# Seven ff tiles in the first pass instead of six, and a margin in the plan ahead of TensorE, in a fused attention and feed-forward kernel

## The chip, the core and the metric

The kernel runs on one NeuronCore of a Trainium2 chip. The metric is the device time of one execution in microseconds. The kernel before takes 1096.32 us, the median of three runs (1095.8 to 1097.32).

## What is computed

Eight batches of eight heads, 576 positions, head dimension 64: banded causal attention (a window of 128 keys) with a linear position bias, then a feed-forward layer over the 4608 tokens with 512 model columns and 2048 ff columns. All in float32.

```python
scores = scale * np.matmul(q, k.transpose(0, 1, 3, 2))
mask = (rel >= 0) & (rel < window)
scores = np.where(mask, scores + bias[None], -1000000000.0)
attn = np.exp(scores - max) / sum
x = (attn @ v).transpose(0, 2, 1, 3).reshape(B * S, H * D)
h = x @ w_in
sp = np.maximum(h, 0.0) + np.log1p(np.exp(-np.abs(h)))
out = (h * erf(sp)) @ w_out
```

## The kernel before

**Attention.** The 64 heads are 32 pairs, counted from 0 (`pair = 4 * batch + g`). A pair has five score groups (`QTILES`), three in its first span and two in its second; the first eight pairs do all first spans before the second ones. For each group TensorE makes the scores `s` (L520, plain fp32, in the early spans; L531, split operands, later), VectorE adds the bias and finds the row's extreme (`p<-s`, L542), ScalarE exponentiates (L552), VectorE inverts the sums (`st`, L570), GpSimd scales `p` (L577), TensorE transposes it (`t`, L595), VectorE or ScalarE copies it out of PSUM, TensorE multiplies it by the values (`px`, L613), and the result `xs` is stored to `xd` in DRAM, and for the first two chunks also kept on chip. Apart from the early first spans, which borrow two more, `s` has a single PSUM buffer: a score group can start only when VectorE has read the one before. The operands of a late pair are split into two parts first (`kh`, `kl`, `a`: L472 to L489) on VectorE, ScalarE and GpSimd.

**Feed-forward.** The tokens are 12 chunks of 384 columns, the 2048 ff columns 16 tiles of 128. One unit is one tile for one chunk: 12 products into `h` (L795), a copy to `hs`, the activation in rounds of four units on ScalarE (L826), the products and the split on VectorE (L836, L840), and 9 products into `o` (L855). There are 192 units. The output accumulates over the ff tiles, and not all weights fit on chip while attention runs, so there are two passes: the first takes the first `NF1` ff tiles for all chunks and stores its sums to DRAM; the second takes the rest, reads these sums back and adds them. The first pass is the filler between attention's instructions; its chunk can begin once attention has finished the batches that the chunk holds (chunk 9 needs batch 6; chunks 10 and 11 need batch 7). `xr` is the chunk loaded back, `xh` and `xl` its two parts (L777 to L781, L770).

**Weights.** Each ff tile of `w_in` and `w_out` arrives as 64-bit words (`wri`, `wro`) and is turned into two float32 parts (`whi`, `wli`, `who`, `wlo`) by a chain on ScalarE and VectorE (L684 to L704). Here "a weight tile" is one ff tile of one of the two. Those of the first pass are prepared while attention runs; those of the second live, all but two tiles of each, in the memory that attention gives back.

**The order.** Nothing is scheduled by the compiler. `Plan` lists every operation with its cost on the engines that could take it, an urgency `at` and its dependencies, walks through time, and hands each engine that is free the most urgent operation that is ready; that gives each engine its fixed order, which the chip then follows with semaphores. `hop` is the time that the planner lets pass between the end of an operation and the start of one that depends on it. `at` of a unit of the first pass grows by `TM` per unit, and `TM` is made from `NF1` such that the pass keeps its length: 4.80 us a unit with six tiles, 4.11 with seven. At the start, 40 small products on a zero tile (`warm`, L399) have the least urgency and fill TensorE's gaps.

Of the kernel before, what the change touches and what calls it, by code (L numbers as in the profile page):

```python
# [26 lines left out]
NTT = CH // P  # L27
LOG_EXP_SET = "natural_log_exp_and_others"

NF1 = 6  # L30
FIT = 8
UPR = (4, 4)
TAIL = (2, 2)
EARLY = 16
# [10 lines left out]
LL, LP, LT = 15, 6, 0  # L45
TM = 1.2 * TA * 20 / (1.5 * NF1)
LEAD = 70
# [84 lines left out]
class Plan:  # L132
# [7 lines left out]
    def hop(self, src, dst):  # L140
        if src == "PE":
            return 0.0 if "PE" in dst else 0.2
        return 0.2 if "Pool" in dst else 0.14

    def __init__(self):
        self.ops = []
# [562 lines left out]
class Moe:  # L709
# [4 lines left out]
    def __init__(self, tc, plan, ctx, x_dram, part_dram, out):  # L714
# [11 lines left out]
        self.rounds = []  # L726
        for n, size, tail in zip((NF1, NF - NF1), UPR, ((), TAIL)):
            n = n * nch - sum(tail)
# [157 lines left out]
def tile_kernel(ctx, tc, qT, kT, vb, w_in, w_out, bias, out, nb=B):  # L886
# [24 lines left out]

    n1 = nch * NF1
    t0 = LEAD
    t1 = t0 + n1 * TM
    w1 = Weights(nc, plan, lambda k, f: (w1p, f"{k}_{f}"), stage, w_in, w_out, range(NF1))
    for k in range(2):
        for f in range(NF1):
            w1.prepare(k, f, t0 - W1A + (f * W1C + W1B * k) * TM)
# [11 lines left out]
    for o in ops:  # L930
        o.outs.append(last)
    pool2 = lambda: w2p[0]
    place = lambda k, f: (
        (pool2, f"{k}_{f}") if f < NF1 + FIT else (w1p, f"{k}_{f - NF1 - FIT}")
    )
# [43 lines left out]
```

## Time and profile before

| | before |
|---|---|
| median of three runs | 1096.32 us |
| profiled execution | 1095.57 us |
| its span, first to last instruction | 1093.8 us |
| mean granted TensorE clock | 0.994 |
| DMA | 109.51 MB, 100 GB/s over the span |

A row of the table of stages reads: stretch in us, its length, then for TensorE (PE), its weight loads (PEld), VectorE (DVE), ScalarE (ACT) and GpSimd (POOL) the busy time and the count of instructions, then the granted TensorE clock, the share of the DMA engines and GB/s. A row of waits reads: engine, what waited and its line, what it waited for, total us, times, the longest. A row of the timeline reads: start, length, engine, line, operation, result and operands; in brackets the idle time ahead of it and what ended it. A busy TensorE is not one at its peak, since its products overlap in the record.

### The profile page before, as it was taken

The page shows a single profiled execution, that of the slowest core. Times are in us where ns is not written, and L with a number is a line of the kernel's source. Part 1 is how long each engine was busy: PE and PEld are TensorE (multiplying, and loading weights), DVE is VectorE, ACT ScalarE, POOL GpSimd, SP SyncE. Part 2 cuts the span into 40 slices and gives each one's busy share as a digit, 9 for nine tenths or more (in the row PEclk, how much of TensorE's full clock was granted, in tenths as well). Part 3 has the DMA queues.
Part 4 walks back from the last instruction along what each step waited for, and adds up shares of the span by engine and source line. Part 5 has one row for each costly group of instructions (what it writes and reads, how often), then busy time and mean ns, then how long its engine had stood idle before and what let it go on. Part 6 is the DMA issues. An engine that isn't in the chain of part 4 may idle for free.

```text
span 1093.8 us, 16894 instructions
## 1 busy us (share of the span) xinstructions
PE 1065.1 (97%) x6000; PEld 975.3 (89%) x6000; DVE 677.9 (62%) x1531; ACT 676.2 (62%) x1393; POOL 289.6 (26%) x438
## 2 busy tenths in 40 slices
PE   7998999999999989999999999999999999999998
PEld 7987889988999989899999998999999999999996
DVE  2789999878887787764888873433333334343342
ACT  4766887776777677765766663645535545445461
POOL 5645657565545555441100000000000000000000
PEclk9998999999999999999999999999999999999999
DMA  6553644646453453412434411220210210202102
GB/s 177 148 157 111 179 132 122 197 110 173 132 138 106 130 157 98 134 34 88 135 117 131 149 61 46 87 63 24 87 58 29 87 54 34 87 19 68 58 17 71
DMA packets 88260, 109.51 MB, mean 100 GB/s; under 512 B 45808, under 2 KB 58224, under 8 KB 88176
## 3 DMA queue, kind: packets, MB, share of 16 engines
q1 hardware_dynamic: 88176, 108.42, 33.6%
q8 instruction: 48, 0.79, 0.3%
q14 instruction: 36, 0.29, 0.1%
HBM read 80.08 MB, written 28.31 MB: 99 GB/s over the span
## 4 chain that ended last, share of the span: by engine, by line
PE 86%; DVE 5%; DMA 3%; POOL 3%; issue 1%; SPq 0%; ACT 0%; POOLq 0%; DVEq 0%
PE o L855 34%; PE h L795 34%; PE px L613 7%; PE t L595 5%; PE s L531 4%; POOL p L577 3%; PE s L520 2%; DMA xr<-xd 1%; DVE p L542 1%; DVE a_None L489 1%; DMA a<-q_t 1%; DMA kz<-k_t 1%; DMA wri<-w_in 1%; DVE hs L836 1%; DVE kl_None L486 0%
## 5 line engine op out<-in xcount | busy, mean ns | idle before, releaser
L795 PE MATMUL h<-xh,whi 128*128 128x384 f32 x768 | 263.9, 344 | 0.7 <-DVE xh L781 0.5
L795 PE MATMUL h<-xh,wli 128*128 128x384 f32 x768 | 260.0, 339 | 0.5 <-DVE wli L704 0.5
L795 PE MATMUL h<-xl,whi 128*128 128x384 f32 x768 | 259.1, 337 | 0.9 <-DVE xl L770 0.9
L855 PE MATMUL o<-who,gh 128*128 128x512 f32 x576 | 228.1, 396 | 0.0
L855 PE MATMUL o<-who,gl 128*128 128x512 f32 x576 | 227.5, 395 | 0.0
L855 PE MATMUL o<-wlo,gh 128*128 128x512 f32 x576 | 227.1, 394 | 0.0
L577 POOL TENSOR_SCALAR p<-p,st 128x256 f32<-128x256 f32 (+2 forms) x320 | 197.3, 635 | 95.2 <-DVE st L570 94.2
L777 ACT COPY hs<-h 128x384 f32<-128x384 f32 x113 | 53.8, 477 | 233.7 <-PE h L795 233.2
L552 ACT ACTIVATE p<-p,st 128x256 f32<-128x256 f32 (+2 forms) x320 | 149.0, 468 | 33.4 <-DVE st L542 32.9
L781 DVE COPY hs<-h 128x384 f32<-128x384 f32 x79 | 43.8, 555 | 192.6 <-PE h L795 192.4
L795 PEld LDWEIGHTS h<-xh,whi 128*128 128x128 f32 x768 | 145.4, 189 | 8.6 <-DVE xh L781 0.9
L795 PEld LDWEIGHTS h<-xl,whi 128*128 128x128 f32 x768 | 145.3, 189 | 7.5 <-DVE xl L770 1.1
L795 PEld LDWEIGHTS h<-xh,wli 128*128 128x128 f32 x768 | 144.8, 189 | 1.0 <-DVE wli L704 1.0
L542 DVE CUSTOM_DVE_ANT_0 p<-s,bias_sb 128x256 f32<-128x256 f32 (+2 forms) x320 | 108.8, 378 | 40.4 <-PE s L531 16.1
L855 PEld LDWEIGHTS o<-who,gl 128*128 128x128 f32 x576 | 108.0, 188 | 23.3
L855 PEld LDWEIGHTS o<-wlo,gh 128*128 128x128 f32 x576 | 108.3, 188 | 16.1
L855 PEld LDWEIGHTS o<-who,gh 128*128 128x128 f32 x576 | 108.4, 188 | 15.4
L836 DVE TENSOR_TENSOR hs<-s,hs 128x768 f32<-128x768 f32 x96 | 90.9, 970 | 23.6 <-ACT s L826 23.5
L840 DVE TENSOR_TENSOR gl<-hs,gh 128x768 fp32r<-128x768 f32 x96 | 90.8, 963 | 0.7 <-ACT gh L777 0.6
L595 PE MATMUL t<-ident,p 128*128 128x128 f32 x544 | 82.1, 276 | 6.6 <-POOL p L577 6.2
L595 PEld LDWEIGHTS t<-ident,p 128*128 128x128 f32 x544 | 64.6, 143 | 17.1 <-POOL p L577 9.8
L826 ACT ACTIVATE s<-s 128x768 f32<-128x768 f32 x96 | 76.0, 839 | 0.6
(78 smaller groups left out, 1486.3 us busy)
## 6 DMA issues: line engine op xcount, KB each, us to landing
xr<-xd SPq DMA_DIRECT2D x22, 768.0 KB, 4.3
kr_None<-k_t SPq DMA_DIRECT2D x48, 288.0 KB, 4.3
pd<-ot SPq DMA_DIRECT2D x36, 256.0 KB, 3.6
ot<-pd SPq DMA_DIRECT2D x36, 256.0 KB, 3.0
wri<-w_in SPq DMA_DIRECT2D x16, 512.0 KB, 4.3
wro<-w_out SPq DMA_DIRECT2D x16, 512.0 KB, 3.7
out_dram<-ot SPq DMA_DIRECT2D x32, 256.0 KB, 2.1
qr_None<-q_t SPq DMA_DIRECT2D x24, 288.0 KB, 4.3
```

Source lines behind the costliest of these rows:

```text
L542: nc.vector.tensor_tensor_reduce(out=pt[:m, c0:c1, j, :], in0=blocks(ps[:m, j, :n]), in1=blocks(self.bias[:m, c0 * 64 : c1 * 64]), scale=- ...
L552: nc.scalar.activation(dst, dst, AF.Exp, bias=low[:m, j : j + 1], scale=-1.0, accum_out=total[:m, j : j + 1],)
L577: nc.gpsimd.tensor_scalar(dst, dst, totals[t][:m, j : j + 1], 1.0, op0=ALU.mult, op1=ALU.mult)
L595: nc.tensor.matmul(ps[:, col : col + P], lhsT=p[t][:, kb].rearrange("p j d -> p (j d)"), rhs=self.ident[:, :], is_transpose=True, start=no ...
L613: self.nc.tensor.matmul(dst[:, q0 - base : q1 - base], lhsT=v[:, blk], rhs=sb[sbi][:, off : off + q1 - q0], start=(blk == order[0][0]), st ...
L777: self.nc.scalar.copy(out, src)
L781: self.nc.vector.tensor_copy(out, src)
L795: nc.tensor.matmul(ps[:, :CH], lhsT=ww[:, cs], rhs=xx[:, k], start=(k2 + k + n == 0), stop=(k2 + k + n == 4),)
L826: A.activation(s[:, :n], s[:, :n], AF.Erf)
L836: op({"DVE": dve(n2)}, lambda e, s=s, hs=hs, n=n: V.tensor_tensor(hs[:, :n], s[:, :n], hs[:, :n], ALU.mult), r=[s, hs], w=[hs], at=at)
L840: op({"DVE": dve(n2)}, lambda e, gh=gh, gl=gl, hs=hs, n=n: V.tensor_tensor(gl[:, :n], hs[:, :n], gh[:, :n], SUB), r=[hs, gh], w=[gl], at=at)
L855: nc.tensor.matmul(po.all, lhsT=g[:, j, cs], rhs=w.all, start=(u["start"] and n == 0), stop=(u["end"] and n == 2),)
```

## The change

`NF1` goes from 6 to 7, so the first pass has 84 units and the second 108 (72 and 120 before); 14 weight tiles are prepared under attention and 18 for the second pass (12 and 20). `FIT` goes from 8 to 7: seven ff tiles of the second pass lie in the memory that attention gives back, and two in the places of the first pass's tiles 0 and 1, as before. And the planner lets 0.6 us more pass between an operation of any other engine or a DMA and a TensorE operation that depends on it. The margin is in the plan alone; no instruction waits for it.

```diff
-NF1 = 6
-FIT = 8
+NF1 = 7
+FIT = 7
...
     def hop(self, src, dst):
         if src == "PE":
             return 0.0 if "PE" in dst else 0.2
-        return 0.2 if "Pool" in dst else 0.14
+        return 0.2 if "Pool" in dst else 0.14 + 0.6 * ("PE" in dst)
```

Every engine's order is new from its first rows on. Three places matter below. First TensorE, at the first two score groups of pair 26 (`s26_0`, `s26_1`, `s26_2` are its groups, `px24_1` a product of pair 24). Before, the third group comes directly behind the second:

```order
L613 MATMUL px24_1_4971<-pb24_4953,vbd0_160 128x64
L531 MATMUL s26_1_4983<-kh26_None_0_4759,a26_None_0_4783 128x256
L531 MATMUL s26_1_4983<-kl26_None_0_4836,a26_None_0_4783 128x256
L531 MATMUL s26_1_4983<-kh26_None_1_4785,a26_None_1_4806 128x256
L531 MATMUL s26_1_4983<-kl26_None_1_4852,a26_None_1_4806 128x256
L531 MATMUL s26_2_5010<-kh26_None_0_4759,a26_None_0_4783 128x256
```

and now transposes of pair 25 and products `o` follow the second group, and the third comes only behind a whole unit's `h`:

```order
L531 MATMUL s26_1_5206<-kl26_None_1_5007,a26_None_1_4956 128x256
L595 MATMUL t25_1_0_5213<-ident_62,p25_4_5111 128x128
L595 MATMUL t25_1_0_5213<-ident_62,p25_3_5081 128x128 x2
L595 MATMUL t25_1_0_5213<-ident_62,p25_4_5111 128x128
L595 MATMUL t25_1_0_5213<-ident_62,p25_3_5081 128x128
L855 MATMUL o1_35_4640<-who5_1794,gh40_4906 128x512
L855 MATMUL o1_35_4640<-wlo5_1807,gh40_4906 128x512
L855 MATMUL o1_35_4640<-who5_1794,gl40_4921 128x512
L855 MATMUL o2_35_4667<-who5_1794,gh40_4906 128x512
```

Second GpSimd, at the cast of chunk 9 (`xh9`), before:

```order
L577 TENSOR_SCALAR p28_4_5509<-p28_4_5509,st28_1_5474 128x3x64 x2
L779 TENSOR_SCALAR xh9_0_5693<-xr9_1_5635 128x768
L476 TENSOR_SCALAR a31_None_0_5712<-qr31_None_5601 64x576
L476 TENSOR_SCALAR kh31_None_1_5720<-kr31_None_5580 128x576
L476 TENSOR_SCALAR a31_None_1_5728<-qr31_None_5601 64x576
L779 TENSOR_SCALAR gh44_5762<-hs44_5427 128x768
```

and now:

```order
L476 TENSOR_SCALAR kh31_None_1_5964<-kr31_None_5788 128x576
L476 TENSOR_SCALAR a31_None_1_5976<-qr31_None_5810 64x576
L779 TENSOR_SCALAR xh9_0_5990<-xr9_1_5895 128x768
L577 TENSOR_SCALAR p29_3_5918<-p29_3_5918,st29_1_5919 128x4x64 x2
L577 TENSOR_SCALAR p29_4_5947<-p29_4_5947,st29_1_5919 128x3x64 x2
L779 TENSOR_SCALAR gh54_6091<-hs54_5812 128x768
```

The operands of pair 31 stood behind the cast and now stand ahead of it. Third VectorE near the start, behind the sixth score group (`p1_2`), before:

```order
L542 ISA p1_2_281,st1_0_260<-s1_2_263,bias_sb_63 128x4x64
L542 ISA st1_0_260 128x1
L570 RECIPROCAL st0_0_227<-st0_0_227 128x6
L542 ISA p2_0_308,st2_0_309<-s2_0_300,bias_sb_63 128x2x64
L542 ISA st2_0_309 128x1
```

and now, with the steps of the first weight tile (`wti0`, `wqi0`) between the two score groups:

```order
L542 ISA p1_2_280,st1_0_259<-s1_2_262,bias_sb_63 128x4x64
L542 ISA st1_0_259 128x1
L687 TENSOR_SCALAR wti0_290<-wqi0_232 128x512
L689 SCALAR_TENSOR_TENSOR wti0_290<-wqi0_232,wti0_290 128x512
L570 RECIPROCAL st0_0_226<-st0_0_226 128x6
L691 TENSOR_SCALAR wqi0_232<-wti0_290 128x512
L542 ISA p2_0_311,st2_0_312<-s2_0_300,bias_sb_63 128x2x64
```

## The prediction

> **What bounds the kernel now.** I read the page's totals first, then a table of stages, then the waits of TensorE, and last the chain of waits and the timeline at single stops.
>
> ```profile
> span 1093.8 us, 16894 instructions
> PE 1065.1 (97%) x6000; PEld 975.3 (89%) x6000; DVE 677.9 (62%) x1531; ACT 676.2 (62%) x1393; POOL 289.6 (26%) x438
> ```
>
> TensorE (PE) is busy for 97% of the span; what it waits for is at most 28.7 us. The stages come from the last attention product on TensorE and from a table with PE, weight loads, VectorE, ScalarE and GpSimd, then the granted clock:
>
> ```profile
> L613 PE MATMUL px<-pb,vbd x320: 218/275/377, 68.2 to 502.7; 128*128 128x64 f32 x64, 128*128 128x128 f32 x64, 128*128 128x192 f32 x32
> ...
> 0.00:60.00 60.00, 54.28 (x354) 51.69 (x354) 32.00 (x140) 35.62 (x133) 34.44 (x79) 0.97 0.57 155
> 60.00:100.00 40.00, 32.85 (x191) 28.98 (x190) 34.15 (x95) 27.04 (x71) 20.47 (x31) 0.92 0.56 152
> 100.00:150.00 50.00, 48.70 (x304) 45.20 (x303) 47.96 (x112) 38.78 (x93) 29.81 (x35) 1.00 0.52 148
> 150.00:503.00 353.00, 343.15 (x2225) 319.45 (x2224) 275.34 (x775) 255.94 (x706) 192.86 (x283) 1.00 0.46 127
> 503.00:1071.00 568.00, 568.00 (x2855) 515.35 (x2855) 283.96 (x406) 314.36 (x388) 11.97 (x12) 1.00 0.22 72
> ```
>
> Attention ends at 503 us. Behind it TensorE is busy for 568.00 of 568 us: nothing can be won there except by less work. Ahead of it PE sits idle 5.72, 7.15, 1.30 and 9.85 us, 24.0 in all, and the half clock costs a further 0.03 x 60 + 0.08 x 40 = 5.0 us there. The rest of the 28.7 is the tail, which ends in the same order as before. So a change of order can win at most some 29 us, all in the first 503.
>
> [...]
>
> **The part that is moved.** One unit is one ff tile of one chunk: 12 products h and 9 products o. In the chain of waits a unit looks like this (start, length, line, count):
>
> ```profile
> 700.21 2.10 PE h L795 x12
> 702.31 2.08 PE o L855 x9
> ```
>
> That is 2.10 + 2.08 = 4.18 us a unit, for 192 units before and after. How many lie inside attention now:
>
> ```profile
> 0.00:503.00 503.00, 136.35 (x660) 114.97 (x660) 0.99 0.48 134
> ...
> 0.00:503.00 503.00, 120.03 (x439) 76.33 (x440) 0.99 0.48 134
> ```
>
> The first row is L795, the second L855: 660 / 12 = 55 units of h and 439 / 9 = 48.8 of o. In the new order 756 and 504 products stand ahead of the last attention product, so 63 and 56 units. Inside attention that adds 8 x 2.10 + 7.2 x 2.08 = 31.8 us, and the same 31.8 us leave the stage behind it, which is full either way. **Term 1: 0 us.** Attention would end near 535 us. What could change is only how often TensorE stops on the way there, because the same attention work is now spread over 32 us more of filler.
>
> The changeover costs nothing either: 21 units (84 - 63) of the first pass remain behind attention, 17 before, so 87.8 us of cover instead of 71.1, and 18 weight tiles must be prepared under it instead of 20. If that cover failed, one late tile would hold a unit, 3.6 us of VectorE's time each, as worked out below.
>
> **The stops.** TensorE's waits from 100 to 503 us, and below the dots from 0 to 100 (total, times, longest):
>
> ```profile
> PE s L531 <- DVE st L542: 4.8, 2, 2.8
> PE t L595 <- POOL p L577: 4.5, 7, 1.3
> ...
> PE s L520 <- DMA kz<-k_t: 4.7, 1, 4.7
> PE s L520 <- DVE st L542: 3.4, 3, 1.8
> PE t L595 <- POOL p L577: 1.8, 3, 1.0
> PE s L520 <- issue: 1.4, 1, 1.4
> ```
>
> *Transposes waiting for GpSimd* (L595): 6.3 us in ten waits, 0.63 us each. The new margin lets a product be placed 0.6 us later behind its producer, so by size it could remove nearly all of them. I check that in the order: priced at the cadence of the rows (h 0.175 us a product, o 0.231, and likewise the rest), less than 8 us of TensorE work lies between a bank's last score and its transposes at 12 of 108 places of the old order behind the first 60 us, and at 8 of 111 of the new. A third fewer would be -2.1 us, all of them -6.3; were the delays of GpSimd larger than the margin, nothing or +1.5 (two more). **Term 2: -3 us**, nearer to the count, since the margin moves the plan and not the engines.
>
> *Score groups that follow one another on the one PSUM buffer* (L531, L520): the second must wait until VectorE has read the first. These stops in the timeline, with what ended them:
>
> ```profile
> 395.73 0.28 PE L531 MATMUL s<-kl_None,a_None 128*128 128x256 f32 x1
> 398.77 0.35 PE L531 MATMUL s<-kh_None,a_None 128*128 128x256 f32 x1 [2.76 <-DVE st L542]
> ...
> 92.04 0.89 PE L520 MATMUL s<-kz,a 128*128 128x192 f32 x4 [1.83 <-DVE st L542]
> 94.35 2.04 PE L520 MATMUL s<-kz,a 128*128 128x256 f32 x4 [1.43 <-issue]
> ...
> 76.94 0.89 PE L520 MATMUL s<-kz,a 128*128 128x192 f32 x4 [1.07 <-DVE st L542]
> ```
>
> Behind the first 60 us of that work the old order has three places where a group directly follows another on that buffer: the stops of 2.76, 1.43 and 1.07 us, 5.3 us in all, 1.75 each. At the place of 2.76 (pair 26) the new order has six products o and twelve h in between, 3.5 us, and transposes. But it has two such places of its own (pair 8 to 9, and pair 13). Two at 1.75 are 3.5; bounds 2 x 1.07 and 2 x 2.76. **Term 3: -1.8 us**, from -3.2 to +0.2.
>
> *A queue held up by a load.* The other stop of 150 to 503 us, with GpSimd's row, the load in the chain of waits, VectorE's row, and two windows with their clock:
>
> ```profile
> 447.11 7.62 DMA xr<-xd
> ...
> 454.88 0.83 POOL L779 TENSOR_SCALAR xh<-xr 128x768 fp32r<-128x768 f32 x1 [11.17 <-PE s L531]
> ...
> 456.38 1.21 DVE L489 TENSOR_TENSOR a_None<-qr_None,a_None 64x576 fp32r<-64x576 f32 x1 [2.37 <-POOL a_None L476]
> ...
> 458.27 0.36 PE L531 MATMUL s<-kh_None,a_None 128*128 128x256 f32 x1 [2.05 <-DVE st L542]
> ...
> 350.00:400.00 50.00, 47.06 (x309) 43.99 (x308) 40.74 (x119) 36.56 (x111) 29.82 (x47) 1.00 0.47 134
> 450.00:500.00 50.00, 47.95 (x295) 44.91 (x294) 28.82 (x83) 33.50 (x86) 23.98 (x37) 0.97 0.20 65
> ```
>
> GpSimd's cast of chunk 9 waits for a load of 7.62 us; behind it in its queue stands pair 31's query, for which VectorE waits with the bias of pair 30 behind it, and TensorE needs that buffer. It costs 2.05 us and 0.03 x 50 = 1.5 us of half clock. In the new order pair 31's operands stand ahead of the cast, and behind it the scaling of pair 29, which feeds transposes later on. All gone would be -3.5; the same wait elsewhere, 0. **Term 4: -2.5 us.** [...]
>
> **What is added.** First, two weight tiles more to prepare while attention runs, 14 instead of 12, on VectorE (min, median and longest in ns):
>
> ```profile
> L687 DVE TENSOR_SCALAR wti<-wqi x16: 386/418/843, 27.3 to 565.4; 128x512 int32<-128x512 int32 x16
> L689 DVE SCALAR_TENSOR_TENSOR wti<-wqi,wti x16: 677/684/741, 27.8 to 566.2; 128x512 int32<-128x512 int32 x16
> L691 DVE TENSOR_SCALAR wqi<-wti x16: 415/420/545, 33.3 to 567.7; 128x512 int32<-128x512 int32 x16
> L692 DVE SCALAR_TENSOR_TENSOR wqi<-wri,wqi x16: 650/684/714, 34.1 to 568.9; 128x512 f32<-128x512 uint32 x16
> L700 DVE TENSOR_TENSOR wti<-wti,wqi x16: 679/692/798, 37.7 to 569.6; 128x512 f32<-128x512 f32 x16
> L704 DVE TENSOR_TENSOR wli<-wti,whi x16: 672/684/860, 44.2 to 571.8; 128x512 fp32r<-128x512 f32 x16
> ...
> 19.81 0.29 DVE L542 CUSTOM_DVE_ANT_0 p<-s,bias_sb 128x128 f32<-128x128 f32 x1 [7.66 <-PE s L520]
> ```
>
> The six add up to 3.58 us a tile, 7.2 for two. VectorE is free for 5.9 us of 60 to 100 and for only 2.0 us of 100 to 150, so this is where it would hurt. Against that, the new order begins the first tile right behind the sixth score group, in the 7.66 us in which VectorE now waits for the seventh, and has all 14 done by the 47th score group, where the old one has 12 done by the 50th. One tile in the idle stretch leaves 3.6 us for the crowded part, against 7.9 us of room there. From -1 to +7.2; **term 5: +1 us**. The early half clock (0.08 x 40 = 3.2 us) goes if the stops at 92 and 94 us go and comes back with others: **term 6: -1 us**, from -3.2 to 0.
>
> Second, SyncE now issues the query of pair 8 ahead of the keys of pair 2 (pairs count from 0), on which TensorE waits 4.7 us:
>
> ```profile
> 17.85 0.58 SPq L435 DMA_DIRECT2D qr_None<-q_t  x1
> ...
> 23.04 1.11 SPq L422 DMA_DIRECT2D kz<-k_t  x2
> ```
>
> Its 0.58 us of issuing comes ahead of those keys, which wait for TensorE's slot in any case (0), or share the bus with its 128 x 576 x 4 bytes (295 KB at the 155 GB/s of the first 60 us, 1.9 us). **Term 7: +0.6 us.** The third weight load also moves forward on SyncE, where it waits for VectorE's fourth step of the first tile; the keys of pair 4 queue behind it. That step stands just behind the bias of the seventh score group, which ran near 20 us, and the keys are issued at 23.04 us now: 0.
>
> Third, TensorE enters a run of MoE products from an attention product at 171 places, 155 before.
>
> ```profile
> 304.02 0.45 PE L855 MATMUL o<-who,gh 128*128 128x512 f32 x1
> 304.31 0.40 PE L855 MATMUL o<-wlo,gh 128*128 128x512 f32 x1
> ```
>
> Such an entry takes 0.29 instead of 0.231 us, 0.06 more; 16 of them make **term 8: +1 us**.
>
> The sum is 0 - 3 - 1.8 - 2.5 + 1 - 1 + 0.6 + 1 = -5.7 us. The profiled execution took 1095.57 us, its span 1093.8; so 1089.9. The median of the runs shown, 1096.32, lies 0.75 above it: **1090.6 us**, 0.5% faster.
>
> **Rivals.** *The waits only move.* The margin is a number of the planner; the engines keep their latencies, and a new order meets other late loads and queues. For it: pairs 8 and 13 already show the pattern that pair 26 loses, and one slow load of 7.62 us was enough. Against it: fewer close transposes, and VectorE's share of the attention stage falls. Then terms 2 to 4 come back as others: 1096, within 0.2% (2.2 us, about what a measurement of this kernel can tell from no change).
>
> *VectorE becomes the bound, slower.* Place: 60 to 200 us. It is busy for 47.96 of 50 us in 100 to 150. If the 7.2 us of the two tiles and the denser filler find no room, scores wait for VectorE on their one buffer, and each us comes out on TensorE: +7.2 against perhaps -2 of the other terms, 1101.5. It decides once VectorE's share in 60 to 150 us passes about 97% (now 82.1 of 90) and PE idles more than the 8.45 us that it does there now. For it: seven tiles are wanted for the first chunk instead of six. Against it: the early start, and 28 us of VectorE idle in the first 60.
>
> *All stops go.* Terms 2, 3 and 4 at their ends, -6.3 - 3.2 - 3.5, and the early clock with -3.2, less 2.6 of costs: -13.6, so 1082.7. Against it: the order still holds close places.
>
> **Chances.** The forecast (1086 to 1094) 0.55; still faster 0.10; the waits only move 0.20; VectorE as the bound 0.15. So faster 0.65, same 0.20, slower 0.15. The range must take in the same case and the near part of the slower one, and little under 1084: 1084 to 1099.
>
> **What would show it.** Attention ends near 530 us, with 63 and 56 units ahead; behind it PE is again busy without a gap. PE's waits for GpSimd fall from 6.3 to near 3 us, those for VectorE from 8.2 to near 5. No window of 50 us from 100 us on has a clock below 1.00. I would be wrong if PE idles over 24 us ahead of the last attention product, if VectorE passes 97% in 60 to 150 us, or if a gap opens at the changeover.

## The result and the profile after

| | before | changed |
|---|---|---|
| median | 1096.82 us (5 runs, 1095.8 to 1099.38) | 1091.25 us (5 runs, 1090.76 to 1093.01) |
| profiled execution | 1095.57 us | 1093.01 us |
| its span | 1093.8 us | 1091.0 us |

The ratio is 0.9949, with a 95% interval of 0.9935 to 0.9962: 0.5% faster, as forecast (1090.6 us). The profiled execution of the changed kernel is the slowest of its five, 1.8 us above their median, and that of the kernel before lies 1.2 us below its own. So the two traces differ by 2.6 us and the medians by 5.6: the account by stages below explains the smaller figure, and no trace here shows the other 3 us.

The page of the changed kernel, its totals:

```profile
span 1091.0 us, 16860 instructions
PE 1067.0 (98%) x6000; PEld 979.3 (90%) x6000; DVE 679.0 (62%) x1531; ACT 678.6 (62%) x1393; POOL 297.3 (27%) x441
```

TensorE is idle for 1091.0 - 1067.0 = 24.0 us instead of 28.7. Its busy time rose by 1.9 us, though it does the same products. The table of stages says where both come from:

```profile
0.00:60.00 60.00, 53.12 (x336) 50.20 (x337) 37.20 (x143) 32.75 (x120) 35.83 (x79) 0.94 0.61 166
60.00:100.00 40.00, 34.59 (x209) 32.91 (x208) 34.78 (x96) 27.19 (x76) 21.69 (x30) 0.91 0.44 127
100.00:150.00 50.00, 46.97 (x279) 43.29 (x279) 45.98 (x111) 39.34 (x94) 29.20 (x33) 0.93 0.56 153
...
150.00:500.00 350.00, 346.16 (x2215) 322.58 (x2214) 271.46 (x756) 259.43 (x698) 188.24 (x272) 1.00 0.46 126
...
535.00:1068.00 533.00, 533.00 (x2677) 483.30 (x2676) 269.51 (x382) 295.14 (x361) 13.30 (x11) 1.00 0.22 72
```

Behind 150 us PE idles 3.84 us, where it idled 9.85. The half clock around 458 us (a granted clock of 0.50 from 460 to 462 us) is gone, but another stretch of it has come, behind a stop at 213 us (0.50 from 216 to 218):

```profile
200.00:250.00 50.00, 47.06 (x293) 42.95 (x292) 39.43 (x111) 38.98 (x101) 23.71 (x36) 0.97 0.50 139
...
450.00:500.00 50.00, 49.95 (x319) 46.00 (x317) 39.51 (x110) 36.77 (x99) 25.92 (x38) 1.00 0.35 95
```

By the clock column that is 0.03 x 50 = 1.5 us behind 150 us in both kernels, so the gain there is idle time alone. Ahead of 150 us it idles 6.88 + 5.41 + 3.03 = 15.3 us instead of 14.2, and by the clock column the half clock went from 5.0 us to 0.06 x 60 + 0.09 x 40 + 0.07 x 50 = 10.7. So the change wins in the late part of attention and gives some of it back early.

TensorE's waits, above the dots from 0 to 150 us, below from 150 to 535:

```profile
PE s L520 <- DMA kz<-k_t: 5.8, 1, 5.8
PE t L595 <- POOL p L577: 5.4, 1, 5.4
PE s L531 <- DVE st L542: 1.7, 1, 1.7
PE o L855 <- ACT who L777: 1.3, 1, 1.3
...
PE s L531 <- DVE st L570: 2.1, 2, 1.9
PE t L595 <- POOL p L577: 0.9, 2, 0.7
PE h L795 <- DVE xl L770: 0.8, 1, 0.8
```

The ten waits of transposes for GpSimd were 6.3 us. There are three now, and again 6.3 us, since one of them is 5.4. What stands around that one, by the timeline (TensorE, GpSimd, VectorE, ScalarE):

```profile
85.76 0.34 PE L795 MATMUL h<-xh,wli 128*128 128x384 f32 x1
91.50 1.33 PE L595 MATMUL t<-ident,p 128*128 128x128 f32 x5 [5.41 <-POOL p L577]
...
87.57 3.88 POOL L577 TENSOR_SCALAR p<-p,st 128x256 f32<-128x256 f32 x4 [2.73 <-DVE st L570]
...
87.31 0.17 DVE L570 RECIPROCAL st<-st 128x4 f32<-128x4 f32 x1
...
90.47 0.69 DVE L704 TENSOR_TENSOR wli<-wti,whi 128x512 fp32r<-128x512 f32 x1
...
81.94 1.28 ACT L828 ACT_TABLE_LOAD   x1
83.27 0.32 ACT L495 COPY xs<-px 128x192 f32<-128x192 f32 x1
...
84.04 0.46 ACT L552 ACTIVATE p<-p,st 128x192 f32<-128x192 f32 x1
...
85.91 0.20 ACT L569 ACTIVATE st<-st 128x4 f32<-128x4 f32 x1
```

The exponentials begin only at 84 us, behind ScalarE's first activation round and a copy; the first sums are ready at 86.1 us (ScalarE's L569), but VectorE's reciprocal comes only at 87.31, behind steps of a weight tile and of the activation in its queue; four scalings on GpSimd take 3.88 us. The next weight tile that TensorE could use as filler (`wli`, L704) is ready at 91.2 us. Whether a unit of an older tile could have stood there was not tested.

### The profile page after: what moved, and what is told of

The parts are those of the page before. It is cut to its first block, busy times and chain, and to the rows that moved or that the text cites. A ratio compares the mean times of both kernels' runs of the same rounds, so it can differ in the third digit from the quotient of the medians.

```text
span 1091.0 us, 16860 instructions
## 1 busy us (share of the span) xinstructions
PE 1067.0 (98%) x6000; PEld 979.3 (90%) x6000; DVE 679.0 (62%) x1531; ACT 678.6 (62%) x1393; POOL 297.3 (27%) x441
## 4 chain that ended last, share of the span: by engine, by line
PE 93%; DMA 3%; DVE 1%; POOL 1%; SPq 0%; ACT 0%; issue 0%; ACTq 0%; POOLq 0%; DVEq 0%
PE h L795 36%; PE o L855 36%; PE px L613 8%; PE t L595 6%; PE s L531 5%; PE s L520 3%; POOL p L577 1%; DMA wri<-w_in 1%; DMA xd<-xs 1%; DMA xr<-xd 0%; DMA kz<-k_t 0%; DMA qr_None<-q_t 0%; PE warm_ps L399 0%; DVE p L542 0%; DVE a_None L489 0%
## 5 line engine op out<-in xcount | busy, mean ns | idle before, releaser
L777 ACT COPY hs<-h 128x384 f32<-128x384 f32 x119 | 56.5, 478 | 241.3 <-PE h L795 240.7
L781 DVE COPY hs<-h 128x384 f32<-128x384 f32 x73 | 40.6, 556 | 198.5 <-PE h L795 198.3
L840 DVE TENSOR_TENSOR gl<-hs,gh 128x768 fp32r<-128x768 f32 x96 | 93.4, 991 | 1.3 <-ACT gh L777 1.0
L779 POOL TENSOR_SCALAR xh<-xr 128x768 fp32r<-128x768 f32 x7 | 7.5, 1075 | 262.3 <-DMA xr<-xd 123.0
```

What stands on the lines that cost most here:

```text
L777: self.nc.scalar.copy(out, src)
L781: self.nc.vector.tensor_copy(out, src)
L840: op({"DVE": dve(n2)}, lambda e, gh=gh, gl=gl, hs=hs, n=n: V.tensor_tensor(gl[:, :n], hs[:, :n], gh[:, :n], SUB), r=[hs, gh], w=[gl], at=at)
```

## Experiments

All times are medians; each ratio is to runs of the kernel before on the same chip. The kernels e1 to e4, e5 to e8, e9 to e11, and e12 ran on four chips, where the kernel before had medians of 1097.87, 1097.43, 1097.61 and 1096.6 us, so kernels of different groups are compared by their ratios. The idle time of TensorE is length less PE's busy time in the table of stages of one profiled execution.

| kernel | median us | ratio to before, 95% interval | idle 0 to 60 | 60 to 150 | 150 to 500 | 500 to 700 |
|---|---|---|---|---|---|---|
| before | 1096.82 | | 5.72 | 8.44 | 9.85 | 0 |
| changed | 1091.25 | 0.9949 [0.9935, 0.9962] | 6.88 | 8.44 | 3.84 | 0 |
| e1: seven tiles, no margin | 1097.75 | 0.9994 [0.9981, 1.0007] | 5.73 | 14.44 | 2.95 | 0 |
| e2: six tiles, margin 0.6 | 1099.25 | 1.0014 [1.0001, 1.0027] | 7.54 | 9.92 | 5.47 | 0.45 |
| e3: seven, 0.3 | 1101.47 | 1.0039 [1.0024, 1.0054] | 5.93 | 12.81 | 8.19 | 0 |
| e4: seven, 1.0 | 1087.88 | 0.9918 [0.9897, 0.994] | 7.50 | 8.88 | 4.34 | 0 |
| e5: changed, query behind keys | 1090.68 | 0.9939 [0.992, 0.9958] | 6.34 | 8.26 | 3.64 | 0 |
| e6: changed, two weight steps out | 1090.76 | 0.9941 [0.9921, 0.9962] | 8.01 | 7.14 | 3.18 | 0 |
| e7: changed, no tables | 1092.52 | 0.9956 [0.9938, 0.9975] | 7.53 | 8.50 | 4.03 | 0 |
| e8: before, cast behind | 1093.83 | 0.9968 [0.9954, 0.9983] | 5.78 | 7.63 | 9.11 | 0 |
| e9: six, 2.0 | 1104.09 | 1.0063 [1.004, 1.0086] | 7.52 | 10.58 | 2.80 | 9.02 |
| e10: seven, 2.0 | 1090.95 | 0.9945 [0.9928, 0.9961] | 7.62 | 7.73 | 3.17 | 0 |
| e11: seven, 1.0, query behind | 1086.70 | 0.9899 [0.988, 0.9917] | 5.91 | 8.72 | 1.39 | 0 |
| e12: seven, 0.8, query behind | 1086.19 | 0.9905 [0.9885, 0.9925] | 5.76 | 9.22 | 0 | 0 |

### The parts apart: tiles and margin

Seven tiles without the margin (e1); six with it (e2); seven with half of it and with more (e3, e4).

```diff
 e1
-        return 0.2 if "Pool" in dst else 0.14 + 0.6 * ("PE" in dst)
+        return 0.2 if "Pool" in dst else 0.14
 e2
-NF1 = 7
-FIT = 7
+NF1 = 6
+FIT = 8
 e3 and e4: 0.3 and 1.0 in place of 0.6
```

> Seven tiles in the first pass, the planner without the margin. Theory (the gain is the margin's: the move of units is worth nothing, term 1, and transposes wait on GpSimd as before): about 1096, within 3 us of the kernel before; TensorE waits for GpSimd's scaled p in about ten places, 5 to 9 us; idle time of TensorE from 150 us to attention's end 8 to 12 us. Rival (the gain is the seven tiles': more filler lets TensorE ride over late producers): about 1091, waits as in the changed kernel.

> Six tiles as before, the margin of 0.6 us in the plan. Theory (the margin's gain): about 1091 to 1092, waits of transposes for GpSimd down to two to four places. Rival (the seven tiles'): about 1096. Second rival (any new order is a new draw): anywhere from 1089 to 1099, with stops at new places.

> Seven tiles, half the margin (0.3 us). If the margin works by its size, the time lies between that of no margin and 1091.25, about 1093 to 1094, with some five waits for GpSimd. If it is a new draw each time, there is no such order.

> Seven tiles, a margin of 1.0 us. If the margin works by its size, the short waits are gone already at 0.6 and the time is 1090 to 1091.5; if too large a margin makes the plan hold TensorE's products back and the filler run out, 1093 or more, with more places where score groups follow each other directly. New draw: anywhere from 1088 to 1097.

Neither part alone gains anything: e1 stands at the time of before, e2 slightly above it. The theory that the margin alone brings the gain falls with e2, and so does the one for the seventh tile with e1. That the two work together is not shown by this alone, since each kernel also has an order of its own; over all runs below, the four margins from 0.6 to 2.0 us gained with seven tiles, and the two tried with six, 0.6 and 2.0, did not. What e1 does is seen in two stages of its table:

```profile
60.00:150.00 90.00, 75.56 (x425) 68.12 (x425) 74.29 (x191) 59.09 (x155) 43.28 (x58) 0.89 0.51 142
150.00:500.00 350.00, 347.05 (x2227) 323.57 (x2227) 275.58 (x754) 263.06 (x698) 196.53 (x274) 1.00 0.46 128
```

With the seventh tile alone the late stage is already as good as in the changed kernel (2.95 us idle), but 14.44 us are lost between 60 and 150, in single stops, and the granted clock of that stage is 0.89, where the changed kernel has 0.92. Nor is the late stage good in every order with seven tiles: e3 idles 8.19 us there. The margin of 0.3 is the slowest of the seven-tile kernels, that of 1.0 the fastest of these four. The size of the margin does not order them. What they idle from 60 to 500 us sets e3 (21.0 us) and e1 (17.4) apart from the changed kernel (12.3) and e4 (13.2), but does not explain the order of these last two.

### Term 4 by itself: a queue held up by a load

One instruction of the kernel before is moved on GpSimd, by a helper that takes an operation behind another in the finished order, with what depends on it:

```diff
+        for o, behind in [(("xh", 9, 0), ("a", 39, 1))]:
+            order = self.later(order, self.mark[o], self.mark[behind])
         for o in order:
             self.emit(o)
```

> The kernel before with one instruction moved on GpSimd: the cast of chunk 9 stands behind the scaling of pair 31's query and keys instead of ahead of it. All other engines keep their order. Theory (term 4 is a queue held up by a load): the stop of 2.05 us near 456 us and the half clock behind it are gone, and the time falls by 2 to 3.5 us against the kernel before, ratio 0.997 to 0.998. Rival (the stop only moves, to the products of chunk 9 or to the transposes behind it): another stop of 1 to 2 us in 440 to 480 us, and the time within 1 us of the kernel before.

The timeline of GpSimd and of TensorE there, then the stage (lines are shifted by some ten: L486 is L476 of before, L793 is L779):

```profile
452.84 0.83 POOL L486 TENSOR_SCALAR a_None<-qr_None 64x576 fp32r<-64x576 f32 x1 [8.78 <-PE s L541]
...
456.11 1.49 POOL L793 TENSOR_SCALAR xh<-xr 128x768 fp32r<-128x768 f32 x1
...
464.68 0.44 PE L605 MATMUL t<-ident,p 128*128 128x128 f32 x2 [0.82 <-POOL p L587]
...
450.00:500.00 50.00, 49.18 (x312) 45.75 (x312) 29.41 (x83) 34.53 (x88) 25.32 (x37) 1.00 0.23 74
```

Pair 31's query no longer stands behind the load, the stop of 2.05 us is gone, and the clock of that window is 1.00 instead of 0.97. The stage keeps one short wait of 0.82 us. The time falls by 3.6 us (1097.43 to 1093.83, by the interval 1.9 to 5.0). By the traces the window from 450 us gains 2.05 - 0.82 = 1.2 us of idle time and 1.5 us of half clock, 2.7 us together. Term 4's mechanism is shown, and its 2.5 us and its upper end of 3.5 both lie in the interval.

### Term 7: the query ahead of the keys

The same helper moves the load of pair 8's query on SyncE behind the keys of pairs 2 and 3, in the changed kernel (e5) and with a margin of 1.0 (e11):

```diff
+        for o, behind in [(("q", 8, None), ("k", 3, 0))]:
+            order = self.later(order, self.mark[o], self.mark[behind])
```

> The changed kernel with one instruction moved on SyncE: the load of pair 8's query is issued behind the keys of pairs 2 and 3 instead of ahead of them. All other engines keep their order. Theory (term 7 was too small): the scores of pair 2 begin near 18.6 us again instead of 20.1, TensorE's wait for those keys falls from 5.8 us to near 4.7, and the time falls by 1 to 1.5 us, to about 1090. Rival (the load's place is covered by the wait for TensorE's slot, or the clock's windows decide): the wait stays above 5.5 us and the time within 0.5 us of the changed kernel.

> Seven tiles with a margin of 1.0 us, and the load of pair 8's query behind the keys of pairs 2 and 3 on SyncE, all other engines in the order of that kernel. Theory (term 7, 0.5 us by the run of the changed kernel with the same move): TensorE's wait for the keys of pair 2 falls from 6.2 us to near 5.5, and the time by 0.5 us, to 1087.4. Rival: no difference.

SyncE's issue of the query in the changed kernel, then the load of pair 2's keys in the chain of waits, from issue to landing, in the changed kernel, in e5 with its wait, and in the kernel before:

```profile
12.65 1.42 SPq L435 DMA_DIRECT2D qr_None<-q_t  x1
...
15.05 4.90 DMA kz<-k_t
```

```profile
12.00 7.49 DMA kz<-k_t
...
PE s L531 <- DMA kz<-k_t: 5.3, 1, 5.3
```

```profile
11.90 6.54 DMA kz<-k_t
```

With the query out of the way the keys are issued 3 us earlier, but their load takes 7.49 us instead of 4.90, and the scores of pair 2 start only 0.5 us earlier, at 19.62 us instead of 20.08. The kernel before issues these keys at nearly the same time as e5 and starts the scores at 18.58. So by these traces the query's place accounts for 0.5 of the 1.5 us by which the start is late, and what slows the keys' load in e5 stays open. With a margin of 1.0 the wait falls by more, from 6.2 us (e4) to 4.1 (e11). But e6 and e7, which keep the changed kernel's order, wait 6.5 us where it waits 5.8, so 0.7 us lie between executions of one order. The medians of e5 and of the changed kernel differ by 0.57 us, less than their intervals tell apart; those of e11 and e4 by 1.2, with intervals that overlap. The direction is as expected; a gain in time is not shown.

### The stop of 5.4 us

Two of the six VectorE steps of a weight tile are left out (e6), or the activation rounds of the first pass are replaced by copies (e7), with all orders kept:

```diff
 e6
-        for fast, dst, emit in steps:
-            op({"DVE": dve(DM, fast)}, lambda e, emit=emit: emit(), r=[raw, q, t], w=[dst], at=at)
+        for n, (fast, dst, emit) in enumerate(steps):
+            op({"DVE": dve(DM, fast)}, lambda e, n=n, emit=emit: n == 1 or emit(), r=[raw, q, t], w=[dst], at=at)
...
 e7
+            if first:
+                for us, n, n2, hs, s, at in pairs:
+                    A.copy(s[:, :n], hs[:, :n])
+                return
```

> The changed kernel without two of the six VectorE steps of every weight tile (the sign, L689, and the sum, L700), so 1.38 us less of VectorE for each of the 14 tiles prepared inside attention; the weights are then not the reference's. Every order is kept. Theory V (VectorE's weight steps, and GpSimd running slower beside them, make the stops between 60 and 150 us): the stop of 5.4 us at 86 us falls below 3, GpSimd's scaling of 128x256 in 60 to 150 us falls from a mean of 0.88 us to 0.75 or less, PE is busy for at least 84 of those 90 us instead of 81.6, and the time falls to 1085 to 1087. Rival A (ScalarE's first activation round, 7 us with its table loads, makes that stop): it stays above 4.5 us and the time within 1.5 us of the changed kernel.

> The changed kernel with the activation rounds of the first pass replaced by plain copies: no table loads and no second activation, so about 7 us less of ScalarE a round; the activation of the first pass is then left out of the result. Every order is kept. Rival A (ScalarE's round ahead of the exponentials makes the stop at 86 us): the exponentials run at 80 us instead of 84, the stop of 5.4 us is gone or below 1, PE is busy for at least 85 of the 90 us from 60 to 150, and the time falls to 1083 to 1086. Theory V (VectorE's weight steps make it): the stop stays above 3 us and the time falls by less than 3.

Both fall short. The waits for GpSimd and, in e7, ScalarE's timeline, for e7 and then e6:

```profile
PE t L595 <- POOL p L577: 6.3, 3, 5.4
...
76.02 1.56 ACT L825 COPY s<-hs 128x768 f32<-128x768 f32 x2
83.26 0.32 ACT L495 COPY xs<-px 128x192 f32<-128x192 f32 x1 [5.69 <-PE px L613]
```

```profile
PE t L595 <- POOL p L577: 5.1, 2, 4.4
```

Without tables ScalarE is free at 77.6 us, and still the exponentials begin at 84: the copy of an attention product stands ahead of them in its queue, and TensorE ends that product at 83.2. In the changed kernel the round ends at the same time, 83.2, so each of the two hides behind the other. With less VectorE work the stop is 1.0 us shorter, 4.4 us, PE is busy for 82.86 us of the 90, and the time stays that of the changed kernel; of theory V only the faster scaling on GpSimd came true (714 ns, shown at the end). So the stop is made by a chain of queues with several links late at once, and neither of the two costs makes it alone. What would remove it e6 and e7 do not say.

### Is it the count of close places, and what is the seventh tile for?

The prediction counted places with less than 8 us of TensorE work between a bank's last score and its transposes. Counted again in the same way for these runs, behind the first 60 us, the kernel before has 13 (the prediction said 12), e1 13 and the changed kernel 8. Larger margins leave hardly any such place, with six tiles (e9) and seven (e10); e12 has seven of them.

```diff
-        return 0.2 if "Pool" in dst else 0.14 + 0.6 * ("PE" in dst)
+        return 0.2 if "Pool" in dst else 0.14 + 2.0 * ("PE" in dst)
```

> Six tiles in the first pass, as in the kernel before, with a margin of 2.0 us. Its order has no place behind the first 60 us with less than 8 us of TensorE work between a bank's last score and its transposes (before: 13, changed kernel: 8, seven tiles with a margin of 1.0: 3) and none where a score group directly follows another on its buffer (before: 3, changed kernel: 2). Theory C (these two counts set the stops, whatever the number of tiles): TensorE's waits for GpSimd at L595 fall below 2 us and the time to 1084 to 1089. Rival S (the seventh tile is needed, since it frees the stage behind 150 us): the time stays above 1092.

> The changed kernel with a margin of 2.0 us instead of 0.6: one close place instead of 8, three directly following score groups instead of 2. Theory C: TensorE's waits for GpSimd at L595 fall below 2 us, those for VectorE at L531 stay near 5, and the time is 1086 to 1089, near that of the margin of 1.0. Rival D (a larger margin holds products back, which then meet other late work, so that each order has stops of its own): waits of another kind appear, above 4 us in all, and the time is above 1091.

> Seven tiles with a margin of 0.8 us, between the changed kernel's 0.6 and the 1.0 of the fastest run, and the load of pair 8's query behind the keys, so that only the margin differs from the two runs with that load behind (0.6: 1090.7 us, 1.0: 1086.7 us). Its order has 7 close places behind the first 60 us (0.6: 8, 1.0: 3) and 1 directly following score group (2 and 3). Size theory: the time lies between the two, 1088 to 1089.5. Theory C (the count of close places sets it): 1090, as with 0.6. Rival D (stops of the order's own between 60 and 150 us decide): the time may lie outside 1086.7 to 1090.7, and the difference is found in that stage and not behind 150 us, where PE stays busy for 346 to 349 of 350 us.

With six tiles and 2.0 us attention itself is smooth behind 150 us (2.80 us idle), but a gap opens at the changeover. The stage of e9 and its longest wait from 600 to 700 us:

```profile
500.00:700.00 200.00, 190.98 (x947) 171.98 (x945) 140.01 (x220) 115.10 (x144) 11.48 (x11) 0.97 0.30 97
...
PE o L855 <- POOL who L779: 6.6, 1, 6.6
```

Weights of the second pass come late there: with six tiles 20 of them must be ready when the rest of the first pass runs out, with seven 18, and in no run with seven tiles is there any idle time from 500 to 700 us. The cast of `who` waits there for VectorE's sum (L700), and VectorE is busy for 26.31 of the 30 us from 630 to 660. So with a margin of 2.0 us the tile pays for room at the changeover; that two weight tiles fewer make this room is the likely reason and was not tested apart. With the change's own 0.6 us the place is another: e2 idles 0.45 us there, and the 4.2 us that it idles more than the changed kernel are spread over all four stages (0.7, 1.5, 1.6 and 0.45). Rival S was right in e9's time, not in its reason. Theory C falls: e9 has no close place, idles 20.9 us up to 500 us, where the changed kernel idles 19.2, and is the slowest of all, and e10, with one, has other waits (8.1 us for VectorE at L520) and the time of the changed kernel. e12 says it plainest, with seven close places:

```profile
60.00:150.00 90.00, 80.78 (x483) 73.85 (x482) 79.59 (x204) 66.68 (x167) 49.36 (x65) 0.94 0.52 142
150.00:500.00 350.00, 350.00 (x2268) 328.59 (x2267) 277.26 (x766) 258.91 (x703) 200.71 (x283) 1.00 0.46 127
```

No idle time at all in 350 us, so a close place need not cost anything. Its time, 1086.19 us, lies below those of the margins 0.6 and 1.0 with the same load moved, but by the ratios it stands between them (0.9939, 0.9905, 0.9899), and its interval overlaps both, so the time does not settle the size theory. Rival D named the wrong stage: the margins 0.6, 0.8 and 1.0 with the query behind idle 8.26, 9.22 and 8.72 us between 60 and 150, so that stage does not explain the difference between 1090.7 and 1086.2; the late stage (3.64, 0, 1.39) and the half clock (by the clock column 10.7, 8.7 and 8.9 us ahead of 150 us) do. e12 and e11 are the fastest, 1.0% below the kernel before and 0.5% below the changed one (0.9899 / 0.9949 = 0.995).

## Why the prediction was right, point by point

The time was right to 0.7 us, but not every step.

**Term 1, the part that is moved: right.** The last attention product starts at 531.5 us (535 forecast):

```profile
L613 PE MATMUL px<-pb,vbd x320: 217/275/328, 75.3 to 531.5; 128*128 128x64 f32 x64, 128*128 128x128 f32 x64, 128*128 128x192 f32 x32
```

The order has the 63 and 56 units ahead of it, and behind it TensorE is busy for 533.00 of 533.00 us. No gap opened at the changeover, and e9 shows that the cover worked out there can fail: with that of six tiles and a larger margin, it does.

**Term 2, transposes that wait for GpSimd: right in the late stage, wrong in its sum and in its measure.** The ten waits of the kernel before, first those behind 150 us and then those ahead of it:

```profile
PE t L595 <- POOL p L577: 3.4, 5, 1.3
...
PE t L595 <- POOL p L577: 2.9, 5, 1.0
```

Behind 150 us the five of 3.4 us became two of 0.9, which gains 2.5 us. Ahead of it the five of 2.9 us became one of 5.4, at 86 us, which was not foreseen and takes the 2.5 us back. The term was forecast at -3 us and came to 0. The step that failed is to take the places where "less than 8 us of TensorE work lies between a bank's last score and its transposes" as the measure of these waits: e1 has as many such places as before and idles 2.95 us behind 150, e12 has seven and idles none.

**Term 3, score groups on the one buffer: right in place and size.** The two places named, pair 8 to 9 and pair 13, by the timeline:

```profile
139.20 0.30 PE L531 MATMUL s<-kh_None,a_None 128*128 128x128 f32 x1 [1.66 <-DVE st L542]
...
215.33 0.55 PE L531 MATMUL s<-kh_None,a_None 128*128 128x256 f32 x1 [1.88 <-DVE st L570]
```

They sum to 3.5 us, the forecast value, where the old three took 5.3.

**Term 4, the queue behind the load of chunk 9: right.** The stop and its half clock are gone (0.05 us idle and a clock of 1.00 in the window from 450 us). Against the 2.5 us taken, e8 alone gives 2.7 us by the traces and 3.6 by the medians, with an interval of 1.9 to 5.0.

**Term 5, two more weight tiles: no loss of its own that shows.** VectorE is busy for 34.78 + 45.98 = 80.8 of the 90 us from 60 to 150, against 82.1 before, so it did not become the bound in the form of that rival. The weight steps take part in the stop at 86 us with 1.0 us (e6); e6 leaves out steps of all 14 tiles, so the price of the two that were added was not measured.

**Term 6, the early half clock: wrong sign.** Forecast -1 us, "if the stops at 92 and 94 us go". They went, and one stop of 5.4 us came in their place, with the clock at 0.50 from 90 to 94 us and at 0.54 from 94 to 96, and with more at half the clock than before: by the clock column 10.7 instead of 5.0 us ahead of 150 us. That is an upper bound for the cost, since idle time lies in those windows too; the busy time of TensorE grew by 1.9 us.

**Term 7, the query ahead of the keys: right in sign.** The wait grew by 1.1 us, from 4.7 to 5.8, against 0.6. The query's place is 0.5 of it by e5, near the forecast; the rest stays open, and 0.7 us of such a wait lie between executions of one order.

**Term 8**, the entries into runs of products, was not measured by itself.

So terms 2 to 4, -7.3 us together in the forecast, came to 0, -1.8 and -2.7 to -3.6, some -5. By the traces the late stage gave 6.0 us of idle time and no clock, the early stage took back 1.2 us of idle time, and TensorE's busy time grew by 1.9, which leaves a span shorter by 2.8 us; the medians differ by 5.6, and what makes up the rest is not shown. That the forecast of the time came within 0.7 us is therefore in part luck: term 2 was not there in the sum, and term 6 had the wrong sign. The forecast that no window behind 100 us would fall below full clock failed (0.93 and 0.97). What stays open is why a given order has its stops where it has them between 60 and 150 us: a small change of the margin draws a new order, and there the runs lose between 7.1 and 14.4 us.

## What to carry to other kernels

Test a margin in a planner together with the work that can fill it: here margins of 0.6 us and more gained with seven tiles and not with six. Where the seventh tile helps is seen only for the margin of 2.0 us, at which six tiles leave a wait of 6.6 us at the changeover; that each order is also a draw with stops of its own is not ruled out. Look for stops by queue, not by distance in the order: e12 has seven close places and no stop behind 150 us, while one late instruction that stood ahead in GpSimd's queue was worth 3.6 us (1.9 to 5.0) when it was moved (e8), against 5.6 us for the whole change. At 86 us, where several engines were late to the same point, taking work from one of them showed little: 1.0 of 5.4 us in e6, nothing in e7.

## What the runs showed of the hardware

**GpSimd's scaling is not one price.** The 128x256 form in the stage from 60 to 150 us, in the changed kernel and then in e6:

```profile
L577 POOL TENSOR_SCALAR p<-p,st 128x256 f32<-128x256 f32 x25 | 21.7, 880 | 9.2 <-DVE st L570 9.0
```

```profile
L577 POOL TENSOR_SCALAR p<-p,st 128x256 f32<-128x256 f32 x26 | 18.2, 714 | 9.3 <-DVE st L570 9.1
```

Its mean is 880 ns there and 574 from 20 to 60 us; in the kernel before it is 810 and 509. With two VectorE steps a weight tile left out, and VectorE busy for 69.2 of the 90 us instead of 80.8, it is 714. The planner has a single price for it. What makes it slower from 60 to 150 us no run here isolates.

**The same stop does not always cost the clock.** The stop of pair 13 is 1.88 us in the changed kernel and in e7, which keeps its order. The product behind the stop and the window in e7:

```profile
215.09 0.36 PE L531 MATMUL s<-kh_None,a_None 128*128 128x256 f32 x1 [1.88 <-DVE st L570]
...
200.00:250.00 50.00, 46.86 (x303) 42.73 (x303) 40.18 (x112) 28.81 (x94) 24.67 (x37) 1.00 0.50 138
```

In the changed kernel that product took 0.55 us instead of 0.36, and the window had a clock of 0.97: the clock fell behind the stop in one execution and not in the other. The length of a stop does not tell here whether the half clock follows it. In the changed kernel it followed 1.88 us, with two shorter stops (0.83 and 0.23 us) in the 6 us before; in the kernel before it followed 2.05 us (0.50 from 460 to 462), and e8, without that stop, has a clock of 1.00 in the window; but behind the stop of 2.76 us of the kernel before, which ends at 398.77 us, the clock stayed at 1.00 (396 to 420 us). Part of the spread between executions of one kernel may come from this; that was not tested.
